# One argmax step from VectorE to GpSimd, one addition to ScalarE, and a new order table, in a fused attention and two-layer-pair kernel

## The chip, the cores and the metric

The kernel runs on one core of a Trainium2 chip. The metric is the time of one execution in microseconds on the device, as the median of several runs. The engines are named as in the profile: PE (TensorE matrix multiplication), PEld (its weight loads), DVE (VectorE), ACT (ScalarE), POOL (GpSimd), SP (SyncE, which here only issues DMAs).

## The reference

```python
# q, k, v: (2, 8, 768, 64); centroids: (8, 16, 64); weights 512 x 2048 and 2048 x 512, twice
q_assign = np.argmax(np.einsum('bhsd,hcd->bhsc', q_n, c_n), axis=-1)   # q_n, k_n, c_n: rows divided by their norms
k_assign = np.argmax(np.einsum('bhsd,hcd->bhsc', k_n, c_n), axis=-1)
mask = q_assign[:, :, :, None] == k_assign[:, :, None, :]
scores = scale * np.matmul(q, k.transpose(0, 1, 3, 2))
scores = np.where(mask, scores, -1000000000.0)
scores = scores - np.max(scores, axis=-1, keepdims=True)
attn = np.exp(scores)
attn = attn / (np.sum(attn, axis=-1, keepdims=True) + 1e-09)
out = np.matmul(attn, v)                      # then reshaped to x: 1536 x 512
h = x @ w_in;   x = np.maximum(0.01 * h, h) @ w_out        # first layer pair
h = x @ w_in2;  r = np.maximum(h, 0.0);  out = (r * r) @ w_out2   # second
```

## The kernel before

There are two stages. The **attention** stage works on 8 pairs of heads; a pair has 6 units of 256 query rows, so there are 48 units. The **matmul** stage (functions `g1`, `act`, `g2`, `flush`) does the two layer pairs, with every operand split into a high and a low part, so that each product is three matmuls. Its weights are decoded from 64-bit words by three integer steps on DVE (L125, L131, L138), a copy on ACT and a subtraction on POOL (L150); the first two weight chunks are decoded during the last pair of heads, in pieces that are put behind the table rows of that pair.

A unit of the attention stage goes through these steps. The names are those of the order table, and tiles are named as in the profile.

- S0, S1: scores of two tiles of 128 rows into the tile `S` (PE, L343). In three of the twelve `S` tiles of a pair the dot products of the next pair with its centroids ride along (PE, L252).
- R0, R1: row maxima `nm` (DVE, L366). X0, X1: the exponential `e` and the row sums `r` (ACT, L376).
- RC: 1e-9 is added to the row sums (DVE, L388), and the reciprocal is taken (DVE, L389). N0, N1: `e` times that reciprocal (POOL, L392).
- Ta, Tb, Tc: transposes of `e` into tiles `T` (PE, L405). Ha to Hc: their high part `eh` (ACT, L416). La to Lc: their low part `el` (DVE, L422).
- Va, Vb, Vc: the product with the values into the tile `A` (PE, L440), of which there is one buffer. FC and FA: `A` is copied and added into `xt` (ACT L453, DVE L462). The next unit's first L440 matmul can only start when L462 has read `A`.

Beside the units, each pair prepares the next one: scaling and splitting of q, k and v (POOL, L155, L224, L234, L244), and the cluster of each row. For the clusters, M0 to M2 find each group's largest dot product and mark where it stands (DVE, L273, L274); `desc` multiplies the marks by 16 to 1 (POOL, L279), so that the first of several equal marks is largest; `m2` takes that maximum (DVE, L285); `oh` marks the place that equals it (DVE, L288), which is the last step of the argmax. The marks (tile `ds`, 128x384) are then transposed (PE, L298) and turned into mask rows (ACT, L308). For the first pair these steps run before the loop, for the other seven within it.

The order on PE, DVE, ACT and POOL is written out by hand in the table `PLAN`: row `u % 6` holds what is issued at step u, and `name:lag` does that step for unit `u - lag`. Each engine works through its own instructions in that order and waits where an operand is missing. From `manual.close()` on, a scheduler chooses the order instead; before the change that is after the last unit has entered the table, at step 48.

```python
        if u == NU:
            manual.close()
        p = u // UPP
        for op in PLAN[u % UPP].split():
```

Of the kernel before, what the change touches and what calls it, by code (L numbers as in the profile page):

```python
# [8 lines left out]
F32 = mybir.dt.float32  # L9
F32R = mybir.dt.float32r  # L10
I32 = mybir.dt.int32
AF = mybir.ActivationFunctionType
ALU = mybir.AluOpType
# [5 lines left out]

PLAN = (  # L20
    (
        "ldq@0 FC:4 M0@0 FA:4 Tc:3 X0:0 Hc:3 Ta:2 Lb:3 Ha:2 R1:0 Va:3 M1@0 S0:-1 Lc:3 N1:1 "
        "N0:1 X1:0 Vb:3 La:2 Tb:2 Vc:3 R0:-1 S1:-1 Hb:2 RC:0"
    ),
    (
        "khi@0 M2@0 FC:4 FA:4 Tc:3 desc@0 X0:0 Hc:3 Ta:2 Lb:3 klo@0 Ha:2 R1:0 Va:3 m2@0 "
        "S0:-1 Lc:3 N1:1 N0:1 X1:0 Vb:3 qhi@0 La:2 Tb:2 Vc:3 R0:-1 S1:-1 qlo@0 Hb:2 RC:0"
    ),
    (
        "FC:4 oh@0 FA:4 Tc:3 X0:0 Hc:3 Ta:2 Lb:3 Ha:2 R1:0 Va:3 oTb@0 stb@0 S0:-1 Lc:3 N1:1 "  # L30
        "N0:1 X1:0 Vb:3 La:2 Tb:2 Vc:3 R0:-1 S1:-1 Hb:2 RC:0"
    ),
    (
        "FC:4 FA:4 Tc:3 X0:0 Hc:3 Ta:2 Lb:3 Ha:2 R1:0 Va:3 oTa@0 sta@0 S0:-1 Lc:3 N1:1 N0:1 "
        "X1:0 Vb:3 La:2 vhi@0 Tb:2 Vc:3 R0:-1 S1:-1 Hb:2 RC:0"
    ),
    (
        "FC:4 xhi@0 FA:4 Tc:3 X0:0 Hc:3 Ta:2 Lb:3 Ha:2 R1:0 pl00@0 Va:3 S0:-1 Lc:3 N1:1 N0:1 "
        "X1:0 Vb:3 La:2 Tb:2 Vc:3 R0:-1 S1:-1 xlo@0 Hb:2 RC:0"
    ),  # L40
    (
        "FC:4 FA:4 Tc:3 X0:0 Hc:3 Ta:2 Lb:3 Ha:2 pl01@0 R1:0 scale@1 Va:3 vlo@0 ldv@0 S0:-1 "
        "Lc:3 N1:1 N0:1 pl10@0 X1:0 Vb:3 La:2 Tb:2 Vc:3 R0:-1 pl11@0 S1:-1 Hb:2 RC:0"
    ),
)
DOTS = {(0, 0): 0, (0, 1): 1, (1, 0): 2}
# [3 lines left out]
def attention_moe_moe_kernel(  # L50
# [9 lines left out]
    nc = tc.nc  # L60
    NP, _, _, S = qk.shape
    D = 64
    C = 16
# [5 lines left out]
    NU = NP * 2 * (KC // 2)  # L69
# [10 lines left out]
    const = ctx.enter_context(tc.tile_pool(name="const", bufs=1))  # L80
# [9 lines left out]
    desc = const.tile([128, 24, C], F32, name="desc")  # L90
    for c in range(C):
        nc.gpsimd.memset(desc[:, :, c], float(C - c))
    msc = const.tile([64, 1], F32, name="msc")
    mbi = const.tile([64, 1], F32, name="mbi")
    nc.gpsimd.memset(msc[0:32], BIG)
# [164 lines left out]
    ds_t, m_t = {}, {}  # L260
# [24 lines left out]
        nc.vector.tensor_reduce(out=m_t[p][:, :, 0], in_=ds_t[p], axis=AX.X, op=ALU.max)  # L285

    def one_hot(p):
        nc.vector.tensor_tensor(  # L288
            out=ds_t[p], in0=ds_t[p], in1=m_t.pop(p).to_broadcast([128, 24, C]), op=ALU.is_equal
        )  # L290

    oh_t = {}
# [40 lines left out]
    s_t, e_t, r_t, et_t, a_t, xt_t, n_t = {}, {}, {}, {}, {}, {}, {}  # L333
# [37 lines left out]
    def expo(t):  # L371
        e = ep.tile([128, S], F32, tag="e", name="e")
        if t % 2 == 0:
            r_t[t // 2] = sm.tile([128, 2], F32, tag="r", name="r")
        r = r_t[t // 2][:, t % 2 : t % 2 + 1]
        nc.scalar.activation(  # L376
            out=e.rearrange("p (a b) -> p a b", a=2),
            in_=s_t.pop(t)[:, :, 0:HALF],
            func=AF.Exp,
            bias=n_t.pop(t),  # L380
            scale=1.0,
            accum_out=r,
        )
        e_t[t] = e

    def recip(u):
        r = r_t[u]
        nc.vector.tensor_scalar(out=r, in0=r, scalar1=1e-9, scalar2=None, op0=ALU.add)  # L388
        nc.vector.reciprocal(out=r, in_=r)  # L389

    def norm(t):
        nc.gpsimd.tensor_scalar(  # L392
            out=e_t[t], in0=e_t[t], scalar1=r_t[t // 2][:, t % 2 : t % 2 + 1], scalar2=1.0,
            op0=ALU.mult, op1=ALU.mult,
        )
# [68 lines left out]
    def xsplit(p, part):  # L464
        b, hp = divmod(p, HP)
        sl = slice(b * S, (b + 1) * S)
        if part == 0:
            pool_copy(out=xh[:, hp, sl], in_=xt_t[p])
        else:
            nc.gpsimd.tensor_tensor(  # L470
                out=xl[:, hp, sl], in0=xt_t.pop(p), in1=xh[:, hp, sl].bitcast(F32), op=ALU.subtract
            )
# [28 lines left out]
    rank(0)  # L501
    first_max(0)
    one_hot(0)
    lo(0, 0)
    place(0, 0, 0)
    loads_qk(1)
    for g in range(2):
# [13 lines left out]
        "R1": lambda u: rowmax(2 * u + 1),  # L521
        "X0": lambda u: expo(2 * u),
        "X1": lambda u: expo(2 * u + 1),
        "RC": recip,
        "N0": lambda u: norm(2 * u),
        "N1": lambda u: norm(2 * u + 1),
# [3 lines left out]
    for g, c in enumerate("abc"):  # L530
# [17 lines left out]
        "desc": rank,  # L548
        "m2": first_max,
        "oh": one_hot,  # L550
        "oTa": lambda p: oh_trans(p, 0),
        "oTb": lambda p: oh_trans(p, 1),
# [9 lines left out]
    for u in range(-1, NU + 5):  # L562
        if u == NU - UPP:
            pst.close()
            stg.append(ctx.enter_context(tc.tile_pool(name="stg", bufs=1, side="right", reuse_waits="tile")))
            wpx = ctx.enter_context(tc.tile_pool(name="wpx", bufs=G, side="right", reuse_waits="tile"))
            ring.append((wpx, G))
        if u == NU:
            manual.close()
        p = u // UPP  # L570
        for op in PLAN[u % UPP].split():
            if ":" in op:
                name, lag = op.split(":")
                i = u - int(lag)
                if 0 <= i < NU:
                    unit_ops[name](i)
            else:
                name, ahead = op.split("@")
                q = p + 1 + int(ahead)
                if name in ("xhi", "xlo"):  # L580
                    if 0 <= q - 2 < NP - 1:
                        xsplit(q - 2, name == "xlo")
                elif 0 < q < NP:
                    prep_ops[name](q)
        w = u - (NU - UPP)
        if w >= 0:
            k = len(early)
            for f in early[k * w // UPP : k * (w + 1) // UPP]:
                f()
# [115 lines left out]
    for U in range(len(units) + LAG):  # L705
        if U < len(units):
            m, b, f = units[U][:3]
# [55 lines left out]
```

## Time and profile before

| | us |
|---|---|
| median of 3 runs (lowest, highest) | 831.88 (828.59, 834.40) |
| the profiled execution | 828.47 |
| its span on the core | 826.7 |
| attention stage, until only matmul-stage work is left | about 304 |
| matmul stage from there | about 522 |

Busy time over the span is 788.3 us on PE, 563.2 on DVE, 402.8 on ACT and 283.5 on POOL. These are means over two different stages, so the stretches below are read one by one. A row of a table by stretches gives, after the stretch and its length, the busy us (and the number of instructions) of PE, PEld, DVE, ACT and POOL, an engine without work being left out, and then the granted TensorE clock (1.00 is 2.4 GHz, 0.50 is 1.2 GHz), the DMA share and the GB/s. A row of the timeline gives the start, the length, the engine, line and operation, the output and input tiles, how many instructions are merged, and in brackets how long the engine had been idle and who ended that.

### The profile page before, as it was taken

The page shows a single profiled execution, that of the slowest core. Times are in us where ns is not written, and L with a number is a line of the kernel's source. Part 1 is how long each engine was busy: PE and PEld are TensorE (multiplying, and loading weights), DVE is VectorE, ACT ScalarE, POOL GpSimd, SP SyncE. Part 2 cuts the span into 40 slices and gives each one's busy share as a digit, 9 for nine tenths or more (in the row PEclk, how much of TensorE's full clock was granted, in tenths as well). Part 3 has the DMA queues.
Part 4 walks back from the last instruction along what each step waited for, and adds up shares of the span by engine and source line. Part 5 has one row for each costly group of instructions (what it writes and reads, how often), then busy time and mean ns, then how long its engine had stood idle before and what let it go on. Part 6 is the DMA issues. An engine that isn't in the chain of part 4 may idle for free.

```text
span 826.7 us, 10919 instructions
## 1 busy us (share of the span) xinstructions
PE 788.3 (95%) x4143; PEld 680.9 (82%) x4143; DVE 563.2 (68%) x827; ACT 402.8 (49%) x701; POOL 283.5 (34%) x242
## 2 busy tenths in 40 slices
PE   6898898998988899999999999999999999999998
PEld 6798898898988787888888888888888888888886
DVE  3599999989999847887676457658527737533333
ACT  3388687777877736444344234354345324312221
POOL 3468766766773722212222022345112102200000
PEclk9599999999999999999999999999999999999999
DMA  6573645536361122212222112102202201100012
GB/s 165 131 163 65 154 94 117 132 90 139 87 128 49 52 101 102 102 58 96 102 102 101 52 52 102 53 13 90 101 1 102 101 1 55 48 1 1 13 38 102
DMA packets 16132, 67.32 MB, mean 81 GB/s; under 512 B 2768, under 2 KB 2768, under 8 KB 10960
## 3 DMA queue, kind: packets, MB, share of 16 engines
q1 hardware_dynamic: 16080, 66.63, 28.1%
q8 instruction: 33, 0.54, 0.3%
q14 instruction: 19, 0.16, 0.1%
HBM read 43.02 MB, written 3.15 MB: 56 GB/s over the span
## 4 chain that ended last, share of the span: by engine, by line
PE 83%; DVE 11%; ACT 2%; POOL 2%; SPq 1%; issue 1%; DMA 0%; DVEq 0%; ACTq 0%; POOLq 0%
PE h L610 32%; PE o L652 31%; PE A L440 6%; PE S L343 6%; PE T L405 5%; DVE el L422 3%; DVE nm L366 3%; PE S L252 2%; DVE ds L288 2%; DVE xt L462 1%; DVE r L388 1%; PE ohT L298 1%; DVE wt L131 1%; ACT eh L416 1%; PE warm L192 1%; ACT xt L453 1%
## 5 line engine op out<-in xcount | busy, mean ns | idle before, releaser
L150 POOL TENSOR_TENSOR wl<-wt,wh 128x1024 fp32r<-128x1024 f32 x32 | 76.8, 2400 | 299.6 <-ACT wh L149 243.3
L610 PE MATMUL h<-xh,wh 128*128 128x512 f32 x384 | 150.6, 393 | 0.5 <-DVE g L624 0.5
L610 PE MATMUL h<-xl,wh 128*128 128x512 f32 x384 | 151.0, 393 | 0.0
L610 PE MATMUL h<-xh,wl 128*128 128x512 f32 x384 | 150.5, 392 | 0.0
L631 DVE TENSOR_TENSOR gl<-g,gh 128x512 fp32r<-128x512 f32 x96 | 95.5, 996 | 47.2 <-ACT gh L630 47.0
L440 PE MATMUL A<-eh,vv 128*128 128x256 f32 x288 | 86.4, 321 | 23.4 <-DVE xt L462 23.4
L392 POOL TENSOR_SCALAR e<-e,r 128x768 f32<-128x768 f32 x96 | 91.3, 963 | 49.0 <-DVE r L389 19.2
L343 PE MATMUL S<-hb 128*128 128x384 f32 (+1 forms) x384 | 97.7, 370 | 7.1 <-DMA hb<-st 2.8
L366 DVE TENSOR_REDUCE nm<-S 128x1 f32<-128x768 f32 x96 | 90.9, 947 | 16.1 <-PE S L252 14.4
L376 ACT ACTIVATE e<-S,nm 128x768 f32<-128x768 f32 x96 | 86.5, 901 | 29.7 <-DVE ds L274 14.0
L422 DVE TENSOR_TENSOR el<-T,eh 128x512 fp32r<-128x512 f32 x144 | 94.2, 680 | 6.1 <-ACT eh L416 5.4
L416 ACT CAST eh<-T 128x512 fp32r<-128x512 f32 x144 | 79.7, 588 | 30.9 <-PE T L405 29.4
L630 ACT CAST gh<-g 128x512 fp32r<-128x512 f32 x96 | 59.7, 622 | 71.6 <-DVE g L627 41.9
L627 DVE TENSOR_TENSOR g<-t 128x512 f32<-128x512 f32 x48 | 39.5, 822 | 74.1 <-ACT t L626 74.0
L610 PEld LDWEIGHTS h<-xh,wh 128*128 128x128 f32 x384 | 72.1, 188 | 17.4 <-DVE g L624 1.0
L610 PEld LDWEIGHTS h<-xh,wl 128*128 128x128 f32 x384 | 72.1, 188 | 16.1
L610 PEld LDWEIGHTS h<-xl,wh 128*128 128x128 f32 x384 | 72.1, 188 | 15.9
L626 ACT ACTIVATE t<-h 128x512 f32<-128x512 f32 x48 | 28.8, 599 | 114.7 <-PE h L610 114.7
L405 PE MATMUL T<-ident,e 128*128 128x128 f32 x576 | 82.1, 279 | 0.7 <-POOL e L392 0.7
L440 PEld LDWEIGHTS A<-eh,vv 128*128 128x128 f32 x288 | 56.7, 197 | 26.7 <-DVE xt L462 26.3
L440 PE MATMUL A<-el,vv 128*128 128x256 f32 x288 | 77.6, 291 | 0.3 <-DVE el L422 0.3
L652 PE MATMUL o<-gl,wh 128*128 128x512 f32 x192 | 75.5, 393 | 0.0
(88 smaller groups left out, 1442.9 us busy)
## 6 DMA issues: line engine op xcount, KB each, us to landing
wraw<-w SPq DMA_DIRECT2D x32, 1024.0 KB, 4.8
hb<-spl SPq DMA_DIRECT2D x16, 576.0 KB, 4.8
hb<-spl SPq DMA_DIRECT2D x48, 192.0 KB, 5.2
rqk<-qk SPq DMA_DIRECT2D x16, 384.0 KB, 4.4
rv<-v SPq DMA_DIRECT2D x8, 384.0 KB, 3.6
out<-ob SPq DMA_DIRECT2D x12, 256.0 KB, 2.1
hb<-st SPq DMA_DIRECT2D x32, 48.0 KB, 3.3
ct<-cen SPq DMA_DIRECT2D x1, 32.0 KB, 1.9
```

The costliest lines, as they stand in the source:

```text
L150: nc.gpsimd.tensor_tensor(out=wl, in0=t, in1=wh.bitcast(F32), op=ALU.subtract)
L343: nc.tensor.matmul(out=s[:, c, 0:HALF], lhsT=hb[0:k, a, i * 128 : (i + 1) * 128], rhs=hb[0:k, b, c * HALF : (c + 1) * HALF], start=(a == 0 ...
L366: nc.vector.tensor_reduce(out=n, in_=s_t[t][:, :, 0:HALF], axis=AX.XY, op=ALU.max, negate=True)
L376: nc.scalar.activation(out=e.rearrange("p (a b) -> p a b", a=2), in_=s_t.pop(t)[:, :, 0:HALF], func=AF.Exp, bias=n_t.pop(t), scale=1.0, ac ...
L392: nc.gpsimd.tensor_scalar(out=e_t[t], in0=e_t[t], scalar1=r_t[t // 2][:, t % 2 : t % 2 + 1], scalar2=1.0, op0=ALU.mult, op1=ALU.mult,)
L405: nc.tensor.transpose(T[:, o : o + 128], e_t[2 * u + b][:, kc * 128 : (kc + 1) * 128], ident)
L416: nc.scalar.copy(out=eh[:, 2 * g : 2 * g + 2, :].rearrange("p a b -> p (a b)"), in_=T_t[u, g])
L422: nc.vector.tensor_tensor(out=el[:, 2 * g : 2 * g + 2, :].rearrange("p a b -> p (a b)"), in0=T_t.pop((u, g)), in1=eh[:, 2 * g : 2 * g + 2, ...
L440: nc.tensor.matmul(out=A, lhsT=w, rhs=m[:, kc, :], start=(kc == 0 and i == 0), stop=(kc == KC - 1 and i == 1),)
L610: nc.tensor.matmul(out=h, lhsT=w[:, ws], rhs=x[:, kk, c], start=(kk == 0 and i == 0), stop=(kk == HP - 1 and i == 2),)
L631: nc.vector.tensor_tensor(out=gl, in0=g, in1=gh.bitcast(F32), op=ALU.subtract)
L652: nc.tensor.matmul(out=outs[o], lhsT=l, rhs=r, start=(first and i == 0), stop=(last and i == 2),)
```

## The change

`oh` for the last seven pairs leaves DVE. POOL subtracts the maximum from the marks and then clamps at -1 and adds 1, which gives 1 where the two were equal and 0 elsewhere. The addition of 1e-9 becomes a step of its own, RE, an activation with a constant tile `eps` as its bias on ACT; RC keeps the reciprocal. The table is new: RC of a unit stands at the head of the following row, FC comes a row earlier, Tc too, and Vb and Vc stand next to each other. At `manual.close()` the scheduler takes over six steps earlier, at step 42, when the last pair begins.

```diff
 PLAN = (
     (
-        "ldq@0 FC:4 M0@0 FA:4 Tc:3 X0:0 Hc:3 Ta:2 Lb:3 Ha:2 R1:0 Va:3 M1@0 S0:-1 Lc:3 N1:1 "
-        "N0:1 X1:0 Vb:3 La:2 Tb:2 Vc:3 R0:-1 S1:-1 Hb:2 RC:0"
+        "ldq@0 Ta:2 X0:0 FA:4 RC:1 Va:3 khi@0 Hc:3 M0@0 Ha:2 R1:0 M1@0 Lc:3 S0:-1 Tb:2 X1:0 "
+        "Vb:3 Hb:2 La:2 RE:0 Vc:3 klo@0 N0:1 R0:-1 M2@0 Lb:2 N1:1 S1:-1 FC:3 Tc:2"
...
     def one_hot(p):
-        nc.vector.tensor_tensor(
-            out=ds_t[p], in0=ds_t[p], in1=m_t.pop(p).to_broadcast([128, 24, C]), op=ALU.is_equal
+        m = m_t.pop(p).to_broadcast([128, 24, C])
+        if p == 0:
+            nc.vector.tensor_tensor(out=ds_t[p], in0=ds_t[p], in1=m, op=ALU.is_equal)
+            return
+        nc.gpsimd.tensor_tensor(out=ds_t[p], in0=ds_t[p], in1=m, op=ALU.subtract)
+        nc.gpsimd.tensor_scalar(
+            out=ds_t[p], in0=ds_t[p], scalar1=-1.0, scalar2=1.0, op0=ALU.max, op1=ALU.add
         )
...
+    def row_sums(u):
+        nc.scalar.activation(out=r_t[u], in_=r_t[u], func=AF.Identity, bias=eps, scale=1.0)
+
     def recip(u):
-        r = r_t[u]
-        nc.vector.tensor_scalar(out=r, in0=r, scalar1=1e-9, scalar2=None, op0=ALU.add)
-        nc.vector.reciprocal(out=r, in_=r)
+        nc.vector.reciprocal(out=r_t[u], in_=r_t[u])
...
-        if u == NU:
+        if u == NU - 6:
             manual.close()
```

On DVE, in the third row of a pair in the middle of the attention stage, the old order has the equality step L288 between the reciprocal and the addition of `A` into `xt`:

```order
L285 TENSOR_REDUCE m_2005<-ds 128x24
L422 TENSOR_TENSOR el<-T,eh 128x512 x2
L366 TENSOR_REDUCE nm<-S 128x1
L388 TENSOR_SCALAR r<-r 128x2
L389 RECIPROCAL r<-r 128x2
L288 TENSOR_TENSOR ds<-ds,m_2005 128x384
L462 TENSOR_TENSOR xt<-A,xt 64x256
L422 TENSOR_TENSOR el<-T,eh 128x512
```

The same place on DVE in the changed kernel, whose line numbers are 2 to 9 higher:

```order
L287 TENSOR_REDUCE m_2474<-ds 128x24
L470 TENSOR_TENSOR xt<-A,xt 64x256
L397 RECIPROCAL r<-r 128x2
L373 TENSOR_REDUCE nm<-S 128x1
L430 TENSOR_TENSOR el<-T,eh 128x512 x2
L373 TENSOR_REDUCE nm<-S 128x1
L430 TENSOR_TENSOR el<-T,eh 128x512
```

L288 and L388 are gone, and the addition into `xt` (now L470) comes before the reciprocal instead of behind it.

On POOL, for the second and third row of a pair, before:

```order
L392 TENSOR_SCALAR e<-e,r 128x768 x4
L155 TENSOR_SCALAR spl<-rqk 128x768
L279 TENSOR_TENSOR ds<-ds,desc 128x384
L234 TENSOR_TENSOR spl<-rqk,spl 128x768
L392 TENSOR_SCALAR e<-e,r 128x768 x2
L155 TENSOR_SCALAR spl<-rqk 128x768
L234 TENSOR_TENSOR spl<-rqk,spl 128x768
L392 TENSOR_SCALAR e<-e,r 128x768 x4
```

and in the changed kernel:

```order
L157 TENSOR_SCALAR spl<-rqk 128x768
L236 TENSOR_TENSOR spl<-rqk,spl 128x768
L281 TENSOR_TENSOR ds<-ds,desc 128x384
L400 TENSOR_SCALAR e<-e,r 128x768 x2
L294 TENSOR_TENSOR ds<-ds,m_2041 128x384
L295 TENSOR_SCALAR ds<-ds 128x384
L400 TENSOR_SCALAR e<-e,r 128x768 x2
```

The two new instructions (L294, L295) stand between two rows' normalisations, and one split of q (L157, L236) and the `desc` step (L281) stand in one row ahead of a normalisation.

On DVE, in the last pair, the decoding of the first weight chunk (L125, L131) stood together ahead of the addition into `xt`:

```order
L366 TENSOR_REDUCE nm<-S 128x1
L388 TENSOR_SCALAR r<-r 128x2
L389 RECIPROCAL r<-r 128x2
L125 TENSOR_SCALAR wt<-wt 128x1024
L131 SCALAR_TENSOR_TENSOR wt<-wraw,wt 128x1024
L462 TENSOR_TENSOR xt<-A,xt 64x256
```

and the scheduler now puts (L127, L133 are the same two steps):

```order
L373 TENSOR_REDUCE nm<-S 128x1
L127 TENSOR_SCALAR wt<-wt 128x1024
L430 TENSOR_TENSOR el<-T,eh 128x512
L133 SCALAR_TENSOR_TENSOR wt<-wraw,wt 128x1024
L470 TENSOR_TENSOR xt<-A,xt 64x256
```

One of the two decoding steps is moved ahead of a low part, and the longer one still stands right ahead of the addition into `xt`.

## Rows read from the trace of the kernel before

**Rows 1.** Busy time by stretches: five pairs, and the matmul stage.

```profile
67.03:228.22 161.19, 147.74 (x1110) 143.98 (x1110) 152.26 (x281) 122.76 (x251) 116.15 (x111) 0.98 0.49 112
...
304.00:815.00 511.00, 510.46 (x2218) 415.96 (x2217) 300.72 (x355) 191.97 (x282) 94.89 (x44) 1.00 0.18 64
```

**Rows 2.** Timeline of DVE, around 196 us and at two later places.

```profile
195.64 0.79 DVE L388 TENSOR_SCALAR r<-r 128x2 f32<-128x2 f32 x1
196.46 0.17 DVE L389 RECIPROCAL r<-r 128x2 f32<-128x2 f32 x1
196.55 2.15 DVE L288 TENSOR_TENSOR ds<-ds,m 128x384 f32<-128x384 f32 x1
...
212.13 0.17 DVE L389 RECIPROCAL r<-r 128x2 f32<-128x2 f32 x1
...
260.49 1.81 DVE L131 SCALAR_TENSOR_TENSOR wt<-wraw,wt 128x1024 int32<-128x1024 int32 x1
```

**Rows 3.** Timeline of POOL around 196 us and at 212 us.

```profile
195.58 0.82 POOL L155 TENSOR_SCALAR spl<-rqk 128x768 fp32r<-128x768 f32 x1
196.49 1.80 POOL L234 TENSOR_TENSOR spl<-rqk,spl 128x768 fp32r<-128x768 f32 x1
...
212.04 1.84 POOL L244 TENSOR_TENSOR vv<-rv,vv 128x768 fp32r<-128x768 f32 x1
```

**Rows 4.** All instructions of three DVE lines: duration in ns, least, median, greatest.

```profile
L288 DVE TENSOR_TENSOR ds<-ds,m x8: 557/2157/2159, 14.5 to 228.2; 128x384 f32<-128x384 f32 x8
L388 DVE TENSOR_SCALAR r<-r x48: 148/161/1384, 32.0 to 283.9; 128x2 f32<-128x2 f32 x48
L389 DVE RECIPROCAL r<-r x48: 165/166/168, 32.1 to 284.1; 128x2 f32<-128x2 f32 x48
```

**Rows 5.** Who waited for whom from 98.78 to 228.3 us: total, times, longest.

```profile
PE A L440 <- DVE xt L462: 10.8, 4, 2.7
```

**Rows 6.** Busy time by stretches: before and after the clock falls near 167 us.

```profile
166.20:167.40 1.20, 1.20 (x9) 1.01 (x10) 1.20 (x2) 0.00 (x0) 1.08 (x2) 1.00 0.75 146
167.50:170.40 2.90, 2.90 (x14) 2.90 (x13) 2.47 (x6) 1.64 (x4) 0.20 (x1) 0.50 0.98 199
```

**Rows 7.** Timeline of PE: starts of groups between two stalls, and one later stall.

```profile
204.46 0.49 PE L298 MATMUL ohT<-ident,ds 128*64 128x128 f32 x3
204.70 0.95 PE L343 MATMUL S<-hb 128*128 128x384 f32 x4
205.49 0.28 PE L440 MATMUL A<-eh,vv 128*128 128x256 f32 x1
...
209.64 0.28 PE L440 MATMUL A<-eh,vv 128*128 128x256 f32 x1
...
216.24 0.51 PE L343 MATMUL S<-hb 128*128 128x384 f32 x2
...
217.76 1.07 PE L405 MATMUL T<-ident,e 128*128 128x128 f32 x8
...
262.81 0.40 PE L440 MATMUL A<-eh,vv 128*128 128x256 f32 x1 [2.54 <-DVE xt L462]
```

**Rows 8.** Groups by line over the whole span: busy us, mean ns.

```profile
L392 POOL TENSOR_SCALAR e<-e,r 128x768 f32<-128x768 f32 x96 | 91.3, 963 | 49.0 <-DVE r L389 19.2 <-PE S L343 8.8 <-DVE m L273 7.1
...
L453 ACT COPY xt<-A 64x256 f32<-64x256 f32 x48 | 17.7, 369 | 5.3 <-PE A L440 4.1
...
L279 POOL TENSOR_TENSOR ds<-ds,desc 128x384 f32<-128x384 f32 x7 | 7.0, 1005 | 31.6 <-DVE ds L274 31.6
...
L200 ACT ACTIVATE n<-ss 128x1 f32<-128x1 f32 x1 | 0.2, 204 | 1.1 <-DVE ss L198 1.1
```

**Rows 9.** Busy time by stretches, from the seventh pair's stall to the last attention work.

```profile
228.22:230.90 2.68, 0.01 (x1) 0.01 (x1) 2.62 (x4) 1.23 (x4) 2.68 (x2) 1.00 0.79 155
230.90:246.00 15.10, 15.10 (x102) 14.59 (x102) 13.26 (x22) 11.84 (x25) 9.83 (x10) 0.89 0.60 120
246.00:284.00 38.00, 30.43 (x210) 28.74 (x210) 34.94 (x61) 28.52 (x57) 20.25 (x18) 0.96 0.20 65
```

More of the change, by code (lines that the diff above doesn't have):

```diff
@@ L21 @@
     (
-        "ldq@0 FC:4 M0@0 FA:4 Tc:3 X0:0 Hc:3 Ta:2 Lb:3 Ha:2 R1:0 Va:3 M1@0 S0:-1 Lc:3 N1:1 "
-        "N0:1 X1:0 Vb:3 La:2 Tb:2 Vc:3 R0:-1 S1:-1 Hb:2 RC:0"
-    ),
-    (
-        "khi@0 M2@0 FC:4 FA:4 Tc:3 desc@0 X0:0 Hc:3 Ta:2 Lb:3 klo@0 Ha:2 R1:0 Va:3 m2@0 "
-        "S0:-1 Lc:3 N1:1 N0:1 X1:0 Vb:3 qhi@0 La:2 Tb:2 Vc:3 R0:-1 S1:-1 qlo@0 Hb:2 RC:0"
-    ),
-    (
-        "FC:4 oh@0 FA:4 Tc:3 X0:0 Hc:3 Ta:2 Lb:3 Ha:2 R1:0 Va:3 oTb@0 stb@0 S0:-1 Lc:3 N1:1 "
-        "N0:1 X1:0 Vb:3 La:2 Tb:2 Vc:3 R0:-1 S1:-1 Hb:2 RC:0"
-    ),
-    (
-        "FC:4 FA:4 Tc:3 X0:0 Hc:3 Ta:2 Lb:3 Ha:2 R1:0 Va:3 oTa@0 sta@0 S0:-1 Lc:3 N1:1 N0:1 "
-        "X1:0 Vb:3 La:2 vhi@0 Tb:2 Vc:3 R0:-1 S1:-1 Hb:2 RC:0"
-    ),
-    (
-        "FC:4 xhi@0 FA:4 Tc:3 X0:0 Hc:3 Ta:2 Lb:3 Ha:2 R1:0 pl00@0 Va:3 S0:-1 Lc:3 N1:1 N0:1 "
-        "X1:0 Vb:3 La:2 Tb:2 Vc:3 R0:-1 S1:-1 xlo@0 Hb:2 RC:0"
-    ),
-    (
-        "FC:4 FA:4 Tc:3 X0:0 Hc:3 Ta:2 Lb:3 Ha:2 pl01@0 R1:0 scale@1 Va:3 vlo@0 ldv@0 S0:-1 "
-        "Lc:3 N1:1 N0:1 pl10@0 X1:0 Vb:3 La:2 Tb:2 Vc:3 R0:-1 pl11@0 S1:-1 Hb:2 RC:0"
+        "ldq@0 Ta:2 X0:0 FA:4 RC:1 Va:3 khi@0 Hc:3 M0@0 Ha:2 R1:0 M1@0 Lc:3 S0:-1 Tb:2 X1:0 "
+        "Vb:3 Hb:2 La:2 RE:0 Vc:3 klo@0 N0:1 R0:-1 M2@0 Lb:2 N1:1 S1:-1 FC:3 Tc:2"
+    ),
+    (
+        "Ta:2 qhi@0 qlo@0 X0:0 FA:4 RC:1 Va:3 Hc:3 Ha:2 desc@0 R1:0 Lc:3 S0:-1 Tb:2 X1:0 "
+        "Vb:3 Hb:2 La:2 RE:0 Vc:3 N0:1 R0:-1 Lb:2 m2@0 N1:1 S1:-1 FC:3 Tc:2"
+    ),
+    (
+        "Ta:2 X0:0 FA:4 pl00@0 RC:1 Va:3 Hc:3 oh@0 Ha:2 R1:0 Lc:3 S0:-1 Tb:2 X1:0 Vb:3 "
+        "pl10@0 Hb:2 La:2 RE:0 Vc:3 oTb@0 N0:1 R0:-1 Lb:2 N1:1 S1:-1 FC:3 Tc:2"
+    ),
+    (
+        "Ta:2 X0:0 FA:4 RC:1 stb@0 Va:3 Hc:3 oTa@0 Ha:2 R1:0 Lc:3 S0:-1 Tb:2 X1:0 sta@0 Vb:3 "
+        "pl01@0 Hb:2 vhi@0 La:2 RE:0 Vc:3 N0:1 R0:-1 Lb:2 xhi@0 N1:1 S1:-1 FC:3 Tc:2"
+    ),
+    (
+        "Ta:2 X0:0 FA:4 RC:1 Va:3 xlo@0 Hc:3 Ha:2 R1:0 Lc:3 S0:-1 Tb:2 X1:0 Vb:3 Hb:2 La:2 "
+        "RE:0 Vc:3 N0:1 R0:-1 Lb:2 N1:1 S1:-1 FC:3 Tc:2"
+    ),
+    (
+        "Ta:2 X0:0 FA:4 RC:1 scale@1 vlo@0 ldv@0 Va:3 Hc:3 Ha:2 R1:0 Lc:3 S0:-1 Tb:2 X1:0 "
+        "Vb:3 Hb:2 pl11@0 La:2 RE:0 Vc:3 N0:1 R0:-1 Lb:2 N1:1 S1:-1 FC:3 Tc:2"
     ),
@@ L92, in attention_moe_moe_kernel @@
         nc.gpsimd.memset(desc[:, :, c], float(C - c))
+    eps = const.tile([128, 1], F32, name="eps")
+    nc.gpsimd.memset(eps, 1e-9)
     msc = const.tile([64, 1], F32, name="msc")
@@ L523, in attention_moe_moe_kernel @@
         "X1": lambda u: expo(2 * u + 1),
+        "RE": row_sums,
         "RC": recip,
```

## The prediction

> **What bounds the kernel now.** I read the busy time by stretches first, then the waits, then the timelines of the engines that wait. In the matmul stage PE is busy 510.46 of 511 us [rows 1]; the change has no instruction there, so I look for its effect only before 304 us.
>
> In the attention stage I take the five pairs from 67.03 to 228.22 us, 32.24 us each [rows 1]. Two engines are nearly full: DVE with 152.26 of 161.19 us, and PE with 147.74. The 13.45 us in which PE is idle are no spread of small gaps. The list of waits from 98.78 us on has one large entry, PE's L440 behind DVE's addition into `xt`, 10.8 us in 4 times, so 2.7 us once a pair [rows 5]. The timelines show why. At 195.64 us L388, which takes 161 ns in the median, takes 0.79 us, because POOL's L155 runs from 195.58 to 196.40; then L288, whose shortest run is 0.557 us and whose median is 2.157, takes 2.15 us while POOL's L234 runs from 196.49 to 198.29 [rows 2 to 4]. The addition into `xt` stands behind both, and PE behind that. After some of these stalls the granted clock is 0.50 for some us, as at 167.50 [rows 6]; over the five pairs it is 0.98 [rows 1], a loss of 2%, or 3.2 us.
>
> So the present pair is 32.24 us, of which 2.69 is the stall and 0.64 the slower clock. What remains is 28.9 us.
>
> **The change, part by part.** *L288 leaves DVE.* This takes 2.16 us per pair from DVE, and with it the stall: behind the reciprocal nothing is left on DVE in the steady pairs that was seen waiting for POOL. The reciprocal does not inherit the wait: it takes 165 to 168 ns in all 48 cases, and at 212.13 us it does so while POOL's L244 runs from 212.04 to 213.88 [rows 2 to 4]. Gain over the five pairs: 13.45 us, and with the gaps the clock's 3.2 us, since the clock falls only after such gaps in this stretch.
>
> *POOL gets two instructions per pair.* The subtraction has the size of L279, 1.005 us; the clamp has one input of 384 elements, half of L392's 768, which takes 0.963, so between 0.48 and 0.96; I take 0.5, as most of POOL's time goes by elements [rows 8]. No row shows POOL reading an operand that is repeated over 16 places; L288 did so on DVE at 0.557 us [rows 4], so I take no surcharge and leave one to a rival. POOL goes from 23.2 us per pair (116.15 over five) to 24.7, inside 28.9. Queued behind the two are the normalisations of that row, for which PE's transposes of the next row wait, and ahead of the mask transposes L298 stand the two themselves. By the order this costs nothing if POOL is not late; the bound is the row before, with L157, L236, `desc` and two normalisations in one row: 0.82 + 1.80 + 1.0 + 1.93 = 5.55 us [rows 3, 8], against a PE row of 4.15 (below), so at worst 1.4 us per pair.
>
> *The 1e-9 goes to ACT.* DVE loses six L388 of 0.161 us, 0.97 per pair, and at least the 0.63 us of waiting at the one before L288 [rows 2, 4]. ACT gains six activations of 128x2. The nearest rows are 0.204 us for 128x1 without a tile as bias and 0.369 for a copy of 64x256 [rows 8]; I take 0.25, nearer to the small one, which makes 1.5 us. ACT goes from 24.6 us per pair (122.76 over five) to 26.1. The reciprocal now waits for ACT, but it stands a row later, and the wait for `A`'s copy ahead of it already comes later in ACT's order.
>
> *The new table.* DVE needs 30.45 - 2.16 - 0.97 - 0.63 = 26.7 us per pair after the change, POOL 24.7, ACT 26.1. What PE needs I read from its starts in a stretch without gaps [rows 7]: one unit from 205.49 to 209.64, 4.15 us; four S matmuls from 204.70 to 205.49 against 1.52 from 216.24 to 217.76 with dot products, so 0.73 more, three times a pair; three mask transposes 0.24, twice. Together 6 x 4.15 + 3 x 0.73 + 2 x 0.24 = 27.6 us, so PE becomes the bound. The pair is then between 27.6 and 28.9, unless the order makes new waits. I take 28.6, nearer to what was measured, because ACT and DVE would be 91% and 93% full and wait for PE and each other in a fixed order. That is another 0.3 per pair, 1.5 us.
>
> *The sixth stall*, at 228.22, costs 2.68 us, and the clock of 0.89 over the 15.1 us behind it 1.7 [rows 9]: 4.3 us back.
>
> *The last pair by the scheduler.* From 246 to 284 us PE is idle for 38.00 - 30.43 = 7.57 us, and a clock of 0.96 costs 1.5 [rows 9]. A large piece is again PE behind the addition into `xt`, 2.54 us at 262.81, with a decoding step of 1.81 us (L131, started at 260.49) ahead of it on DVE [rows 2, 7]. The scheduler moves one step of that decoding away and leaves L131 there, so I take 3 of the 9.1 us; the bounds are all of it, and one more stall of that kind with its share of the clock, 2.5 + 1.9 = 4.4 us lost.
>
> *Nothing* is taken for the 67 us ahead of the stretch, where the pipeline fills, and for one memset more. The sum is 13.45 + 3.2 + 1.5 + 4.3 + 3 = 25.45 us off the profiled execution's 828.47, so 803.0. The median of the runs shown lies 3.4 us above that execution; a forecast of a median takes half of it: **804.7 us**.
>
> A rule speaks against the move. The Trainium skill, GPSIMD Engine Reference, section Engine selection, assigns elementwise work on a tile to VectorE and calls GpSimd about twice as slow for two inputs; section Elementwise — side-by-side cycle accounting gives about 2.6 cycles per element at 1.2 GHz, from which I estimate 0.83 us for 384 elements. The trace has 1.005 for such an instruction against 0.557 for L288 alone, so it agrees, but it also has 2.157 for L288 beside POOL's work. By the rule the step would cost more time after the change than before; by the trace it leaves the engine on whose queue PE waits.
>
> **The rivals.** *PE's floor everywhere* (10%): pairs of 27.6 give 5 x 4.64 = 23.2 us, with 4.3 and all of the last pair's 9.1 it is 36.6 us, so 793.6. For it speaks that PE had no idle time between stalls; against it that four engines would have to fit without a gap.
>
> *Part is given back* (22%): POOL is late in the row with 5.55 us and PE waits 1.4 us more per pair than at 28.6. Pairs of 30.0 give 5 x 2.24 = 11.2, the last pair nothing, so 15.5 us off and 814.7; with one more stall there 819. For it speaks that row's sum, against it that the rows on either side leave POOL time to run ahead.
>
> *The stall only moves* (5%): PE waits the same 2.7 us per pair at the mask transposes L298, which now depend on POOL, so that the first two terms and the sixth stall are not gained. Left are 1.5 + 3 = 4.5 us, 825.7. Against it: the transposes stand at the end of the row, behind two of three A blocks and the next scores.
>
> *Slower* (3%): POOL's subtraction with the repeated operand is far dearer than any row shows, and POOL becomes the bound. A pair is then 23.2 + 0.5 + x. From x = 10.0 us on, ten times L279, the loss eats the 7.3 us gained elsewhere; at x = 14 a pair is 37.7, 5 x 5.46 - 7.3 = 20 us more than now, 850. The rule above is this direction, though at twice the price and not at ten times. Against it: L392 and L279 show no such surcharge for the other kinds of operands.
>
> **How the numbers follow.** The forecast has 60%, as 797 to 809. The range of 794 to 818 takes in most of the first two rivals and leaves out about 2 in 10: the last two (8%), the better half of the first, and the tail of the second. A measurement of this kernel can tell about 1% from no change, that is 823.6 and 840.2. Faster: 60 + 10 + 22 less a tail of 1, 0.91; within 1%: the moved stall and that tail, 0.06; slower: 0.03.
>
> **What would show it.** Right: no PE gap of 2.7 us before the first L440 matmul of a pair's third row, pairs of about 28.6 us, PE's clock at 1.00 between 67 us and the last pair, the reciprocal still at 0.17 us, subtraction and clamp at about 1.0 and 0.5 us. Wrong steps would be seen as PE waiting for POOL's `e` or for `ds`, ACT activations of `r` far above 0.25 us, or more than 9 us of PE idle time in the last pair. The prediction fails if pairs stay above 30 us.

## The result, and the profile after

The changed kernel takes 802.68 us in the median (801.74 to 803.69, 4 runs), the kernel before 832.14. The ratio is 0.965 with a 95% interval of 0.9612 to 0.9688. Its profiled span is 799.9 us against 826.7.

Busy time by stretches of the changed kernel: five pairs, two stretches at the end of the attention stage, and the matmul stage. The columns are those of [rows 1].

```profile
65.23:209.53 144.30, 142.60 (x1111) 139.09 (x1110) 134.58 (x246) 125.28 (x281) 126.93 (x120) 1.00 0.55 125
230.00:256.00 26.00, 21.72 (x153) 19.18 (x152) 25.66 (x39) 22.48 (x47) 16.33 (x12) 1.00 0.12 41
286.00:289.00 3.00, 0.80 (x4) 0.37 (x3) 2.94 (x4) 1.72 (x4) 0.00 (x0) 1.00 0.00 0
289.00:799.00 510.00, 507.09 (x2208) 414.61 (x2207) 300.54 (x356) 186.83 (x275) 88.90 (x41) 1.00 0.18 64
```

The first row answers to the first of [rows 1]. Five pairs take 144.30 us instead of 161.19, 28.86 a pair. PE is idle for 1.7 us in the five pairs instead of 13.45, and its clock stays at 1.00. DVE is busy 26.9 us a pair instead of 30.45, and POOL has come up to 25.4. In the two short stretches near the end of the attention stage PE is still idle for 4.3 and 2.2 us. In the matmul stage PE has next to no idle time, as before: it is busy 507.09 of 510 us.

The next three views are the waits of the changed kernel between 60 and 205 us, and the timeline of DVE and then of PE at the head of a pair's third row. A line of waits gives the total, the number of times and the longest.

```profile
POOL ds L294 <- DVE m L287: 11.0, 5, 2.2
...
PE A L448 <- DVE xt L470: 1.7, 5, 0.3
```

```profile
122.34 0.54 DVE L287 TENSOR_REDUCE m<-ds 128x24 f32<-128x384 f32 x1
122.91 0.43 DVE L470 TENSOR_TENSOR xt<-A,xt 64x256 f32<-64x256 f32 x1
123.36 0.17 DVE L397 RECIPROCAL r<-r 128x2 f32<-128x2 f32 x1
123.56 0.96 DVE L373 TENSOR_REDUCE nm<-S 128x1 f32<-128x768 f32 x1
```

```profile
123.39 0.39 PE L448 MATMUL A<-eh,vv 128*128 128x256 f32 x1 [0.34 <-DVE xt L470]
```

The gap of 2.7 us [rows 5] is one of 0.3. DVE does `m2`, then at once the addition into `xt` and the reciprocal; nothing waits there for POOL. POOL in turn waits 2.2 us for `m2` before its subtraction, so it is not late, as the prediction feared it might be.

All instructions of the four lines that are new or that follow on a removed one (least, median, greatest, in ns).

```profile
L294 POOL TENSOR_TENSOR ds<-ds,m x7: 841/842/844, 36.8 to 209.5; 128x384 f32<-128x384 f32 x7
```

```profile
L295 POOL TENSOR_SCALAR ds<-ds x7: 1493/1494/1496, 37.7 to 210.5; 128x384 f32<-128x384 f32 x7
```

```profile
L394 ACT ACTIVATE r<-r,eps x48: 295/302/332, 30.6 to 258.5; 128x2 f32<-128x2 f32 x48
```

```profile
L397 DVE RECIPROCAL r<-r x48: 144/154/167, 32.4 to 259.2; 128x2 f32<-128x2 f32 x48
```

The subtraction costs 0.84 us, with its repeated operand, so less than L279's 1.005 [rows 8]. The clamp costs 1.49 and not 0.5. The activation costs 0.30 and not 0.25. The reciprocal is as short as before (154 ns in the median, 166 in [rows 4]).

So the time, the pairs and the shape of the profile came out close to the forecast. Which part of the change did it is another question.

### The profile page after: what moved, and what is told of

Read it like the earlier page. It is cut to its first block, busy times and chain, and to the rows that moved or that the text cites. A ratio compares the mean times of both kernels' runs of the same rounds, so it can differ in the third digit from the quotient of the medians.

```text
span 799.9 us, 10996 instructions
## 1 busy us (share of the span) xinstructions
PE 778.2 (97%) x4143; PEld 671.7 (84%) x4143; DVE 537.8 (67%) x772; ACT 407.2 (51%) x749; POOL 297.1 (37%) x257
## 3 DMA queue, kind: packets, MB, share of 16 engines
q1 hardware_dynamic: 16080, 66.63, 29.1%
## 4 chain that ended last, share of the span: by engine, by line
PE 83%; DVE 11%; ACT 2%; POOL 2%; issue 1%; SPq 1%; DMA 0%; DVEq 0%; ACTq 0%; POOLq 0%
PE h L619 33%; PE o L661 32%; PE A L448 5%; PE S L350 5%; PE T L413 5%; DVE el L430 4%; DVE nm L373 3%; PE S L254 1%; ACT e L383 1%; DVE xt L470 1%; DVE ds L276 1%; PE ohT L305 1%; DVE m L275 1%; PE warm L194 1%; ACT eh L424 1%
## 5 line engine op out<-in xcount | busy, mean ns | idle before, releaser
L373 DVE TENSOR_REDUCE nm<-S 128x1 f32<-128x768 f32 x96 | 91.0, 947 | 16.9 <-PE S L254 14.2
L400 POOL TENSOR_SCALAR e<-e,r 128x768 f32<-128x768 f32 x96 | 88.3, 931 | 18.0 <-DVE r L397 12.3
L635 ACT ACTIVATE t<-h 128x512 f32<-128x512 f32 x48 | 28.7, 599 | 113.9 <-PE h L619 113.9
L448 PE MATMUL A<-eh,vv 128*128 128x256 f32 x288 | 79.5, 306 | 3.5 <-DVE xt L470 3.5
L632 ACT ACTIVATE t<-h 128x512 f32<-128x512 f32 x48 | 28.6, 599 | 92.9 <-PE h L619 92.9
L661 PE MATMUL o<-gh,wl 128*128 128x512 f32 x192 | 75.3, 392 | 0.0
L661 PE MATMUL o<-wh,gl 128*128 128x512 f32 x192 | 75.2, 392 | 0.0
```

What stands on the lines that cost most here:

```text
L373: nc.vector.tensor_reduce(out=n, in_=s_t[t][:, :, 0:HALF], axis=AX.XY, op=ALU.max, negate=True)
L400: nc.gpsimd.tensor_scalar(out=e_t[t], in0=e_t[t], scalar1=r_t[t // 2][:, t % 2 : t % 2 + 1], scalar2=1.0, op0=ALU.mult, op1=ALU.mult,)
L448: nc.tensor.matmul(out=A, lhsT=w, rhs=m[:, kc, :], start=(kc == 0 and i == 0), stop=(kc == KC - 1 and i == 1),)
L661: nc.tensor.matmul(out=outs[o], lhsT=l, rhs=r, start=(first and i == 0), stop=(last and i == 2),)
```

## Experiments

A length of a pair below is the distance between the starts of `m2` in the second and the seventh of the preparations within the loop, divided by five; by it the kernel before has 32.24 us and the changed one 28.86. The kernel before spread from 828 to 841 us over the runs behind the ratios; of the edited kernels each spread by 1 to 4 us, but for the last one. Gains in us are taken from the 832.14 us of the result; the runs beside e5 to e8 had a median of 838.95 for the kernel before, so by their ratios the gains of these four are about 4 us larger. Differences of less than about 3 us between kernels are not read as such.

### e1: the addition back on DVE

```diff
-    def row_sums(u):
-        nc.scalar.activation(out=r_t[u], in_=r_t[u], func=AF.Identity, bias=eps, scale=1.0)
     def recip(u):
-        nc.vector.reciprocal(out=r_t[u], in_=r_t[u])
+        r = r_t[u]
+        nc.vector.tensor_scalar(out=r, in0=r, scalar1=1e-9, scalar2=None, op0=ALU.add)
+        nc.vector.reciprocal(out=r, in_=r)
```

> The changed kernel with the addition of 1e-9 back on DVE (L388's instruction ahead of the reciprocal, nothing on ACT). My theory, that the gain is the stall of PE behind DVE's queue and the clock that falls after it, gives this part almost no share: DVE goes from 26.9 to about 28.5 us per pair, PE's own work in the changed kernel is 28.5, so pairs of 28.9 to 29.2 and 803 to 806 us. The rival, that what counts is every us taken from DVE, with its waits for POOL: POOL is now busy 25.4 of 28.9 us, so the addition waits for it in most of six rows a pair, 2 to 3 us, and pairs are about 31, which gives about 815 to 818 us.

Measured: 816.66 us, ratio 0.9793 (0.9752 to 0.9834), pairs of 30.28. The first view is the addition's line in this run, the second one of its instructions with what POOL does then, the third the busy time of five pairs.

```profile
L398 DVE TENSOR_SCALAR r<-r x48: 151/460/965, 33.6 to 271.9; 128x2 f32<-128x2 f32 x48
```

```profile
115.73 1.82 POOL L236 TENSOR_TENSOR spl<-rqk,spl 128x768 fp32r<-128x768 f32 x1
...
116.62 0.96 DVE L398 TENSOR_SCALAR r<-r 128x2 f32<-128x2 f32 x1
```

```profile
66.78:218.20 151.42, 146.74 (x1112) 139.57 (x1111) 147.71 (x277) 120.11 (x251) 126.47 (x120) 1.00 0.53 119
```

An instruction on two elements a row takes 460 ns in the median, up to 965. The one shown ends 0.03 us after POOL's split, and the other three long ones of that pair end as close behind a POOL instruction, so it waits for what POOL is doing. DVE is busy 147.71 of 151.42 us and is the fullest engine again. The rival's time is right, though its pairs of about 31 are not: the addition's move is worth 14 us in the changed kernel, where my sum had at most 1.5.

### e2: the equality back on DVE

```diff
     def one_hot(p):
         m = m_t.pop(p).to_broadcast([128, 24, C])
-        if p == 0:
-            nc.vector.tensor_tensor(out=ds_t[p], in0=ds_t[p], in1=m, op=ALU.is_equal)
-            return
-        nc.gpsimd.tensor_tensor(out=ds_t[p], in0=ds_t[p], in1=m, op=ALU.subtract)
-        nc.gpsimd.tensor_scalar(
-            out=ds_t[p], in0=ds_t[p], scalar1=-1.0, scalar2=1.0, op0=ALU.max, op1=ALU.add
-        )
+        nc.vector.tensor_tensor(out=ds_t[p], in0=ds_t[p], in1=m, op=ALU.is_equal)
```

> The changed kernel with the last argmax step as one equality on DVE, as before, in the new table's place for it (behind the addition into xt and the reciprocal), and ACT keeping the 1e-9. My theory: the stall comes back in part, since DVE waits about 2 us for POOL and a maximum and two low parts are queued behind it, on which PE depends a little later; a PE gap of 1 to 2.7 us per pair, 810 to 822 us. The rival, that only DVE's sum counts: 26.9 + 2.2 = 29.1 against PE's 28.5, 0.3 us per pair more, 804 to 806 us. A second rival, that the order table alone removed the stall, gives the same 804 to 806 with no PE gap.

Measured: 803.38 us, ratio 0.9635 (0.9591 to 0.9679), pairs of 29.25. My theory asked for 810 to 822 and falls. The equality's line, and the timeline of DVE and POOL around one of them:

```profile
L291 DVE TENSOR_TENSOR ds<-ds,m x8: 539/540/557, 13.9 to 211.7; 128x384 f32<-128x384 f32 x8
```

```profile
153.11 0.17 DVE L391 RECIPROCAL r<-r 128x2 f32<-128x2 f32 x1
...
153.19 0.54 DVE L291 TENSOR_TENSOR ds<-ds,m 128x384 f32<-128x384 f32 x1
153.47 1.92 POOL L394 TENSOR_SCALAR e<-e,r 128x768 f32<-128x768 f32 x2 [2.96 <-DVE r L391]
```

It takes about 540 ns each time and never 2.16 us. In the new table POOL has been waiting for the reciprocal for 2.7 us when the equality starts, so there is nothing for DVE to wait for. The step that gave the change its first name could have stayed where it was: the time is the same within the measurement, and PE's longest wait for the addition into `xt` is 0.3 us, so the second rival holds. The pairs are 0.4 us longer. The first rival's sum is not the reason, as DVE is busy 27.4 us a pair and not 29.1; what the reason is was not looked into.

### e3: the equality on POOL, with the old table

The same edit of `one_hot` as in the change, made to the kernel before, and nothing else.

> The kernel before with one edit: the equality of the last seven pairs becomes POOL's subtraction and clamp; the addition stays on DVE, the old table and the old point where the scheduler takes over stay. My theory: the stall of 2.7 us and the clock go in seven places, pairs of about 28.9, 13.5 + 3.2 + 4.3 = 21 us off 832, so 809 to 814 us. The rival, that the new table is what makes room for POOL's two instructions: PE or DVE waits elsewhere instead, pairs stay above 31 and the time above 822 us.

Measured: 845.10 us, ratio 1.0133 (1.009 to 1.0176), pairs of 34.34. It is slower than the kernel before. Waits between 70 and 200 us, and the timeline at one place:

```profile
PE ohT L303 <- POOL ds L293: 11.5, 4, 2.9
```

```profile
176.00 1.82 POOL L234 TENSOR_TENSOR spl<-rqk,spl 128x768 fp32r<-128x768 f32 x1
...
177.77 0.84 POOL L292 TENSOR_TENSOR ds<-ds,m 128x384 f32<-128x384 f32 x1
...
178.71 1.49 POOL L293 TENSOR_SCALAR ds<-ds 128x384 f32<-128x384 f32 x1
...
180.26 0.55 PE L303 MATMUL ohT<-ident,ds 128*64 128x128 f32 x3 [2.87 <-POOL ds L293]
```

The stall moved as the prediction's third rival says. In the old table the mask transposes stand on PE ahead of the next scores, and POOL does a low part of 1.82 us, the subtraction and the clamp before them. PE waits 2.9 us there, in place of the 2.7 us ahead of L440 before. Its granted clock falls to 0.50 in every pair (near 75, 113, 147, 181, 215 and 249 us), in the trace of the kernel before only in every second one (near 103, 168 and 233 us).

### e4: the table to the end of the attention stage

```diff
-        if u == NU - 6:
+        if u == NU:
             manual.close()
```

> The changed kernel with the table kept to the end of the attention stage, as before the change, so that the scheduler takes over at step 48. My theory gave the scheduler's order of the last pair 3 of the 29 us: 804 to 807 us. Rival: it has no share, as the new table spreads the work of the last pair as well, 801 to 803.5 us, or it loses some, below 801.

Measured: 802.09 us, ratio 0.9618 (0.9578 to 0.9658). The scheduler's order of the last pair has no share that can be told.

### e5: the equality behind the addition into xt

```diff
-        "FC:4 oh@0 FA:4 Tc:3 X0:0 Hc:3 Ta:2 Lb:3 Ha:2 R1:0 Va:3 oTb@0 stb@0 S0:-1 Lc:3 N1:1 "
+        "FC:4 FA:4 oh@0 Tc:3 X0:0 Hc:3 Ta:2 Lb:3 Ha:2 R1:0 Va:3 oTb@0 stb@0 S0:-1 Lc:3 N1:1 "
```

> The kernel before with the equality L288 one place later in the table, behind the addition into xt, on DVE as before. If PE's gap comes from what stands behind the equality on DVE, PE is freed about 2 us earlier at that place, the gap shrinks below 1 us and the clock holds, but DVE keeps its 30.5 us per pair: pairs of 30.5 to 31.2, 820 to 826 us. If the wait of the equality for POOL reaches PE by another way (the low parts and maxima behind it), the gap only moves: 829 to 833 us.

Measured, against the kernel before: 825.75 us, ratio 0.9872 (0.9812 to 0.9931), pairs of 31.77. The equality's line and the waits between 70 and 200 us:

```profile
L288 DVE TENSOR_TENSOR ds<-ds,m x8: 557/1600/1602, 14.3 to 227.1; 128x384 f32<-128x384 f32 x8
```

```profile
PE ohT L298 <- DVE el L422: 8.0, 5, 1.6
...
PEld A L440 <- DVE xt L462: 3.4, 4, 0.9
```

The time is in the first range, and the gap ahead of L440 is small, but another one of 1.6 us stands at the next thing that DVE is late with. The pairs are longer than the 30.5 to 31.2 us of that range, and the clock does not hold: it still falls to 0.50 near 71 and 136 us. Moving the addition into `xt` ahead of the equality leaves the equality at 1.60 us, and whatever stands behind it is late instead.

### e6: the new table alone

Both edits of `one_hot` and `recip` and the earlier `manual.close()` are undone; the table stays.

> The new table alone: the equality and the addition both on DVE, the scheduler from step 48. The runs so far gave 803.4 for the equality on DVE, 816.7 for the addition on DVE and 802.1 for the late point. If the three add up: 815 to 818 us, so that the table earns about half of the gain and the addition's move the other half, and the argmax move nothing. If the equality's move is of use where DVE is the bound (as it is with the addition there), DVE has 2 us per pair more than in the second of those runs or at least 0.54: 820 to 830 us.

Measured: 812.37 us, ratio 0.9713 (0.966 to 0.9765), pairs of 30.38. Five pairs, and a line of the waits between 70 and 200 us:

```profile
64.82:216.71 151.89, 147.22 (x1112) 139.64 (x1111) 148.53 (x281) 120.01 (x251) 115.77 (x110) 1.00 0.52 119
```

```profile
PE A L445 <- DVE xt L467: 2.9, 8, 0.5
```

The table alone removes the stall and the falls of the clock between 65 us and the last pair, and leaves DVE full (148.53 of 151.89). It is a little better than either range. It is also 4 us faster than e1, which has the equality on POOL as well, and the scheduler six steps earlier; there the addition took 460 ns in the median, here 170.

### e7: the addition on ACT, with the old table

```diff
+    def row_sums(u):
+        nc.scalar.activation(out=r_t[u], in_=r_t[u], func=AF.Identity, bias=eps, scale=1.0)
+
     def recip(u):
-        r = r_t[u]
-        nc.vector.tensor_scalar(out=r, in0=r, scalar1=1e-9, scalar2=None, op0=ALU.add)
-        nc.vector.reciprocal(out=r, in_=r)
+        nc.vector.reciprocal(out=r_t[u], in_=r_t[u])
...
-        "N0:1 X1:0 Vb:3 La:2 Tb:2 Vc:3 R0:-1 S1:-1 Hb:2 RC:0"
+        "N0:1 X1:0 Vb:3 La:2 Tb:2 Vc:3 R0:-1 S1:-1 RE:0 Hb:2 RC:0"
```

`RE:0` is put ahead of the last `Hb:2` in the other five rows as well.

> The kernel before with the addition of 1e-9 on ACT, put ahead of the last high part in each row of the old table; all else as before. If the addition costs by DVE's time alone, its 2 us per pair (7.86 us of L388 in four pairs) come off where DVE is the bound, and the stall beside POOL's L234 stays: pairs of 30.5 to 31, 820 to 826 us. If the stall is all that counts, the equality begins earlier and waits for the same end of L234: 829 to 832 us.

Measured: 810.62 us, ratio 0.9694 (0.9643 to 0.9746), pairs of 29.47. Both ranges were too high. The timeline of DVE and POOL at the place that [rows 2, 3] show for the kernel before, and a line of the waits between 70 and 200 us:

```profile
154.96 0.83 POOL L157 TENSOR_SCALAR spl<-rqk 128x768 fp32r<-128x768 f32 x1
155.32 0.88 DVE L290 TENSOR_TENSOR ds<-ds,m 128x384 f32<-128x384 f32 x1
...
155.88 2.00 POOL L236 TENSOR_TENSOR spl<-rqk,spl 128x768 fp32r<-128x768 f32 x1
156.23 0.43 DVE L465 TENSOR_TENSOR xt<-A,xt 64x256 f32<-64x256 f32 x1
```

```profile
PE A L443 <- DVE xt L465: 2.3, 4, 0.6
```

Before, the addition waited out POOL's first split and the equality then waited out the second one of 1.8 us. Without the addition the equality itself meets the end of the first split, takes 0.88 us, and runs ahead of the second, which takes 2.00 instead of 1.80. PE's wait falls from 2.7 to 0.6 us, and the granted clock stays at 1.00 over the five pairs. So most of the stall hung on the addition, by the place it stood in, and not only 161 ns.

### e8: POOL's low part elsewhere in the old table

```diff
-        "S0:-1 Lc:3 N1:1 N0:1 X1:0 Vb:3 qhi@0 La:2 Tb:2 Vc:3 R0:-1 S1:-1 qlo@0 Hb:2 RC:0"
+        "S0:-1 Lc:3 N1:1 N0:1 X1:0 Vb:3 qhi@0 La:2 Tb:2 Vc:3 R0:-1 S1:-1 Hb:2 RC:0"
...
-        "N0:1 X1:0 Vb:3 La:2 Tb:2 Vc:3 R0:-1 S1:-1 Hb:2 RC:0"
+        "N0:1 qlo@0 X1:0 Vb:3 La:2 Tb:2 Vc:3 R0:-1 S1:-1 Hb:2 RC:0"
```

> The kernel before with one entry of the table moved: the low part of q (POOL's L234 beside which the equality waits) is issued in the following row behind the two normalisations instead of at the end of its row. If the equality is slow only because L234 runs beside it, it takes 0.55 us in place of 2.16, PE's gap falls from 2.7 to about 1.1 us, and the clock does not fall: 1.6 us in seven places and about 5 us of clock, 815 to 820 us. If the low part then meets another DVE instruction, the wait moves there: 826 to 832 us.

Measured: 815.89 us, ratio 0.9753 (0.9701 to 0.9805), pairs of 30.05. The equality's line, a line of the waits between 70 and 200 us, and five pairs:

```profile
L288 DVE TENSOR_TENSOR ds<-ds,m x8: 537/539/1136, 14.3 to 219.1; 128x384 f32<-128x384 f32 x8
```

```profile
PE A L440 <- DVE xt L462: 5.4, 5, 1.1
```

```profile
65.41:215.68 150.27, 144.88 (x1112) 140.88 (x1111) 144.55 (x282) 122.31 (x251) 115.43 (x111) 1.00 0.54 120
```

Every number of the first expectation came: 0.54 us, a gap of 1.1, the clock at 1.00, the time. With no instruction moved to another engine, one entry of the table takes back some 16 us.

### e9: no addition at all

```diff
     def row_sums(u):
-        nc.scalar.activation(out=r_t[u], in_=r_t[u], func=AF.Identity, bias=eps, scale=1.0)
+        pass
```

> The changed kernel without the addition of 1e-9, on any engine (left out: the 1e-9; the row sums hold exp(0) = 1, so the sum is at least 1). ACT has six activations of 0.30 us less per pair. If PE is the bound of the pair (28.5 us of its own work in 28.86), nothing changes: 801.5 to 803.5 us. If ACT's in-order work shares the bound, up to 1.8 us per pair come off: 790 to 799 us.

Measured: 802.48 us, ratio 0.9622 (0.9571 to 0.9674), pairs of 28.84. ACT's busy time in five pairs falls from 125.28 to 119.67 us and nothing follows:

```profile
65.30:209.48 144.18, 142.49 (x1112) 139.12 (x1111) 134.46 (x246) 119.67 (x251) 126.86 (x120) 1.00 0.55 126
```

ACT is not the bound of the changed pair; PE, with 28.5 us of busy time in 28.84, is the one left, though no run takes work off it.

### e10 and e11: one load earlier, and warm-up products

e10 is the changed kernel with one load earlier; e11 adds warm-up products.

```diff
     loads_qk(0)
     loads_v(0)
+    loads_qk(1)
...
     place(0, 0, 0)
-    loads_qk(1)
     for g in range(2):
         oh_trans(0, g)
         mask_rows(0, g)
+    warm_up(17)
```

> The changed kernel with the second pair's q and k loaded right behind the first pair's v, instead of between the first pair's placements. PE's second gap before the first unit ends with the mask DMA, which is queued behind those two loads from 17.58 us on; it can start about 0.6 us earlier and land without 0.8 MB beside it. If that wait is on the path: 1 to 2.5 us off, 800 to 802 us. If the wait for the placed heads sets the start: 802 to 803.5 us.

> The kernel of the run with the early load, with 17 more warm-up products on PE between the first mask transposes and the first scores, so that PE has no gap of 2.7 us there. In the changed kernel the granted clock falls to 0.5 at 17.8 us and stays there until 38, while PE is busy from 22 to 37. If PE bounds that stretch, up to half of its 14 busy us come back, 4 to 7 us off the kernel with the early load; if the pipeline's filling through ACT and DVE bounds it, 1 to 3 us.

Measured: e10 800.24 us, ratio 0.9601 (0.9554 to 0.9648); e11 798.91, 0.9588 (0.9542 to 0.9634). Between the two intervals no difference is shown.

The timeline of PE at its second wait at the start, in the changed kernel:

```profile
22.11 0.66 PE L350 MATMUL S<-hb 80*128 80x384 f32 x1 [2.73 <-DMA hb<-st]
```

The same timeline in e10:

```profile
19.77 0.66 PE L350 MATMUL S<-hb 80*128 80x384 f32 x1 [0.54 <-DMA hb<-st]
```

The busy time of two stretches at the start of e11:

```profile
16.00:25.00 9.00, 7.70 (x63) 7.39 (x61) 2.41 (x5) 1.76 (x4) 4.07 (x3) 1.00 0.89 180
25.00:36.00 11.00, 9.96 (x38) 8.53 (x38) 7.36 (x14) 6.98 (x16) 6.80 (x7) 0.54 0.97 233
```

PE's wait for the mask ends 2.3 us earlier, and e10 is 2.4 us below the changed kernel, which by itself is less than I read as a difference. e11 is 3.8 us below it. With the warm-up the clock holds at 1.00 until 25.8 us, and falls after a wait of PE for DVE of 1.2 us; most of the filling is at half clock again. The warm-up's own 1.3 us agree with its second expectation, that the filling through ACT and DVE sets the start, but are too small to show it.

### e12: both moves, with the old table

The kernel of e7 with the `one_hot` of the change.

> The old table with both moves: the addition on ACT as in the run that did this alone (810.6 us), and the equality as POOL's two instructions. If the equality's move does its harm by the mask transposes, which stand on PE ahead of the next scores and wait for POOL's clamp, PE waits 1.5 to 3 us per pair there again: 818 to 826 us. If that wait was only there because DVE's addition held POOL up, both moves together are no slower than the addition's alone: 808 to 812 us.

Measured: 840.87 us, ratio 1.0086 (1.0047 to 1.0125), pairs of 33.60. The waits between 70 and 200 us and POOL at one place:

```profile
PE ohT L305 <- POOL ds L295: 14.0, 4, 3.5
```

```profile
138.67 1.82 POOL L236 TENSOR_TENSOR spl<-rqk,spl 128x768 fp32r<-128x768 f32 x1
...
140.45 0.84 POOL L294 TENSOR_TENSOR ds<-ds,m 128x384 f32<-128x384 f32 x1
...
141.38 1.49 POOL L295 TENSOR_SCALAR ds<-ds 128x384 f32<-128x384 f32 x1
```

Beyond both ranges: in the old table the equality's move loses 30 us against e7. The wait is the one of e3, and longer, since PE comes earlier to it: at the places shown PE is ready 3.9 us after `m2` starts, in e3 4.7 us, and POOL is done 7.4 and 7.6 us after it.

## Why the prediction was right, and where it was not

**The bound before** was read rightly. PE's gap comes from DVE waiting for POOL ahead of the addition into `xt`: e8 takes POOL's instruction away from that place, and equality, gap and clock change by the expected amounts.

**"L288 leaves DVE ... Gain over the five pairs: 13.45 us"** is the step that failed, though its size came. The stall went and the clock stayed up; but not because L288 left. With L288 on DVE the changed kernel loses nothing that can be told (e2), and with L288 on POOL and the rest as before it is slower than the kernel before by 13 us (e3). That the forecast came out is luck to this extent: it gave the whole stall to the one part that does not earn it. The prediction costed the new table only by what it left of PE's own work, and not by what it puts beside the equality and ahead of the mask transposes.

**"The 1e-9 goes to ACT"** was priced far too small. It has no term of its own; the sum leaves at most 0.3 us a pair and 1.5 in all for it and the table together. It is worth 14 us in the changed kernel (e1 against the change) and 22 in the old table (e7), that is 1.4 and 2.8 us a pair. I had taken 161 ns and one wait; but its line in the trace of the kernel before has more than twice that in the mean (busy us, mean ns):

```profile
L388 DVE TENSOR_SCALAR r<-r 128x2 f32<-128x2 f32 x48 | 16.1, 336 | 0.0
```

The wait can come in any of the six rows of a pair, with whatever POOL does then, and in the old table it put the equality behind the start of POOL's second split.

The shares of the change are therefore not a sum. By themselves the table is worth 20 us (e6) and the addition 22 (e7), together 29 (e2), as either one takes away most of the same stall, and with both PE is nearly full. The argmax step is worth nothing with the new table and costs 13 to 30 us without it (e3, e12). The scheduler's share, 3 us in the sum, is nothing that can be told (e4).

**PE as the next bound** was right, the pair of 28.6 too: 28.86. That ACT does not hold it there is shown by e9; that PE does is read from its busy time. PE's own need was read too low, though, with 27.6: it is busy 28.5 us a pair with a clock of 1.00, so the rival of PE's floor everywhere could not have come. The five pairs gave 16.9 us where the sum had 18.15.

**The last pair** gave more than its 7.3 us. From the seventh `m2` in the loop to the end it is 591.0 us in place of 601.9, of which I estimate 2 to 3 as the later place of `m2` (it started 3.4 us ahead of DVE's first step of the next row, and now 0.6 us), so 8 to 9 us. As e4 has 592.0, and e6, where DVE keeps both the equality and the addition, 593.5, most of this comes with the table and not with the scheduler or a lighter DVE queue; it was not taken apart further.

**The rivals.** Nothing was given back at POOL, against the second rival: POOL waits for DVE. The moved stall, to which I gave 5% and 825.7 us, is what this change does without its table, at 845.10 (e3) and 840.87 us (e12). In the new table the mask transposes stand on PE behind all three A blocks and one of the two next scores, not behind two blocks and the scores as I had written. The surcharge of the slower rival did not come: the subtraction with its repeated operand takes 0.84 us, and the clamp, which I had at 0.5, takes the 1.49.

**The rule on the engines**, in the Trainium skill, GPSIMD Engine Reference, section Engine selection, keeps such work on VectorE. The runs agree with it here: POOL needs 0.84 and 1.49 us for what DVE does in 0.54 when POOL leaves it alone (e2), and nothing was gained.

## What to carry to other kernels

When an instruction takes four times its shortest duration, look at what the other engine runs at that moment before moving it: here one table entry that kept the two apart was worth 16 us (e8), and the move to the other engine alone was a loss (e3). A tiny instruction that must wait for another engine costs by its place in the queue and not by its length. When several edits each remove the same stall, price them together against the next bound; a sum that comes out right does not show that its terms are.

## What was not expected of the hardware

On POOL a clamp with an addition on 128x384 took 1.494 us, while two multiplications in one instruction on twice the elements (L400) take 0.93 and a subtraction of two tensors of that size 0.842, even with one of them repeated 16 times. Which part of the clamp makes it dear was not tried.

The short reciprocal on DVE took 144 to 167 ns in all 48 cases of the changed kernel, while an addition of the same shape took 151 to 965 ns in e1.
